# Computing, reading and storing the last block of 128 tokens in two column halves

## The chip, the cores and the metric

The kernel runs on one core of one Trainium2 chip. The metric is the device time of one execution in microseconds (us); lower is better. Times are medians of several executions. A ratio of two kernels is the mean time of one kernel's fast runs over the mean of the other's fast runs of the same rounds, so it is not quite the ratio of the medians quoted. "Same" means within 2%. All timed runs here were in the fast state, so nothing below depends on a slow run. Three runs (e6 to e8) are single looks (one profiled run), which are of unknown state for one core; they are used only for the order and the times of events in the last six microseconds.

In this kernel TensorE does the matmuls and writes the sums to PSUM, VectorE reads them from there, and SyncE issues the stores to memory (DMA transfers). A store moves as packets, and a semaphore, a counter that an engine can wait for, is raised after them: the last store of the kernel before is 128 packets of 2 KB, the last of which ended at 1052.30 us; 16 increments of its semaphore landed from 1052.70 to 1053.04. The "granted clock" in the views below is the share of TensorE's full clock that it was granted.

## The reference, cut to what matters

An attention with a feature map gives `x` (4608 tokens of 512 numbers). A mixture of 8 experts follows, and every token goes through all 8, weighted by a balanced table `P`:

```python
out = np.zeros((N, D), dtype=np.float32)         # N=4608, D=512
for e in range(E):                               # E=8 experts, hidden size 1024
    h = np.maximum(x @ w1[e], 0.0)
    ye = h @ w2[e]
    out += P[:, e:e + 1] * ye
```

The change concerns the last `h @ w2[7]`, of the last group of 512 tokens, and there only the last 128 tokens.

## The kernel before

Tokens are worked in nine groups of 512. For expert 7 the order is group 8, then 0 to 7, so group 7 is the last one. For it alone the second product is computed by plain matmuls in four blocks of 128 tokens. Each block is eight matmuls of 128x512 that sum into one bank of PSUM (a `P1` tile of the program, 128x512 FP32), one read by VectorE (`acc = P * bank + acc`), and one store of 256 KB. `pe`, `dve` and `dma` record an operation with an estimated duration and the keys that it reads and writes; a small planner orders the recorded operations, and the framework places the waits.

```python
# ... cut: attention, routing, the fast products of all other groups
    def store(g, ts, one=0):
        if one:
            dma('SP', 1 << 18, 320, lambda: nc.sync.dma_start(
                out=out[g * S:g * S + SM].rearrange('(p j) d -> p j d', j=NJ)[:, ts:ts + 1],
                in_=acc[g][:, ts:ts + 1, :]),
                [('acc', g, ts, j) for j in range(2)], [('out', g, ts)])
        # ... cut: stores of the other groups

    def down8(e, g, hT, w2):

        for ts in (2, 3, 0, 1):
            py = new("P1")                      # a P1 tile in PSUM, 512 columns
            for fc in range(8):
                i, j = fc // 4, ts // 2
                pe(512, lambda py=py, ts=ts, fc=fc: mm(
                    py(), hT[fc // 4]()[:, fc % 4, ts * 128:ts * 128 + 128], w2()[:, fc, :],
                    fc == 0, fc == 7), [...], [py])
            dve(580, lambda py=py, ts=ts: nc.vector.scalar_tensor_tensor(
                out=acc[g][:, ts, :], in0=py(), scalar=P[:, 4 * g + ts, e:e + 1],
                in1=acc[g][:, ts, :], op0=ALU.mult, op1=ALU.add),
                [py, "P"], [("acc", g, ts, j) for j in range(2)])
            store(g, ts, 1)
```

Here `NJ` is 4 and `SM` is 512. In the group's part of the output, partition `p` of block `ts` holds token `4p + ts`. A store of one block therefore writes 128 rows of 2 KB that lie 8 KB apart.

Of the kernel before, what the change touches and what calls it, by code (L numbers as in the profile page):

```python
# [12 lines left out]
ALU = mybir.AluOpType  # L13
# [155 lines left out]
def kernel(  # L169
# [11 lines left out]
    nc = tc.nc  # L181

    B, H, S, D = q.shape
    DF = w_phi.shape[1]
    N, DD = out.shape
    E = moe_w_gate.shape[1]
    FF = moe_w1.shape[2]
    NP = H // 2
    NJ = 4
    SM = 128 * NJ  # L190
# [19 lines left out]
    P = const.tile([128, NT, E], FP32, name="P")  # L210

    NA = 5
    acc = [accp.tile([128, 4, DD], FP32, name=f"acc{g}", tag=f"acc{g}") for g in range(NA)]
# [16 lines left out]
    def pe(cols, fn, r=(), w=(), takes=()):  # L230
        plan.op("PE", max(cols / 2400.0 + 0.0025, 0.032), 0.32, fn, r, w, takes)
# [4 lines left out]
    def dve(el, fn, r=(), w=(), shared=False):  # L236
        plan.op("DVE", el / 960.0 + 0.09, 0.22, fn, r, w, shared=shared)
# [4 lines left out]
    def dma(queue, nbytes, rate, fn, r=(), w=()):  # L242

        plan.op(queue, 0.8 if queue == "POOL" else 0.6, 0.0, fn, r, w, (), nbytes / rate / (125 / 100))
# [43 lines left out]
    def new(tag):  # L288
        return R[tag].new()
# [6 lines left out]
    def load_w(e, r=()):  # L296
        w1, w2 = new("w1"), new("w2")
        for w, src in ((w1, moe_w1), (w2, moe_w2)):
            dma("POOL", 2 << 20, 280, lambda w=w, src=src: nc.gpsimd.dma_start(
                out=w(), in_=src[e].rearrange("(c p) f -> p c f", p=128)),  # L300
                r, [(w, i, j) for i in range(2) for j in range(2)])
        return w1, w2
# [80 lines left out]
    def mm(out_, lhsT, rhs, start, stop):  # L383
        nc.tensor.matmul(out_, lhsT=lhsT, rhs=rhs, start=start, stop=stop)  # L384
# [341 lines left out]
    for i in range(2):  # L726
        dve(64, lambda i=i: nc.vector.tensor_copy(
            out=wphi2[64 * i:64 * i + 64, i, :], in_=wphi_f[64 * i:64 * i + 64, :]),
# [10 lines left out]
    for i in range(2):  # L739
# [5 lines left out]
        out=wgate, in_=moe_w_gate.rearrange("(c p) e -> p c e", p=128)), w=["wgate"])  # L745
# [126 lines left out]
        expert0(i)  # L872


    def store(g, ts, one=0):
        if one:
            dma('SP', 1 << 18, 320, lambda: nc.sync.dma_start(
                out=out[g * S:g * S + SM].rearrange('(p j) d -> p j d', j=NJ)[:, ts:ts + 1],
                in_=acc[g][:, ts:ts + 1, :]),
                [('acc', g, ts, j) for j in range(2)], [('out', g, ts)])  # L880
        elif g < 8:
            if ts % 2:
                dma("SP", 1 << 19, 320, lambda: nc.sync.dma_start(
                    out=out[g * S:g * S + SM].rearrange("(p j) d -> p j d", j=NJ)
                    [:, ts - 1:ts + 1], in_=acc[g][:, ts - 1:ts + 1, :]),
                    [("acc", g, t, j) for t in (ts - 1, ts) for j in range(2)], [("out", g, ts)])
        else:
            for i in range(2):
                b = 2 * ts + i
                rows = slice(i * 64, i * 64 + 64)  # L890
                dma("SP", 1 << 17, 320, lambda b=b, rows=rows: nc.sync.dma_start(
                    out=out[b * S + SM:(b + 1) * S], in_=acc[8][rows, ts, :]),
                    [("acc", 8, ts, j) for j in range(2)], [("out", 8, b)])
# [9 lines left out]
    def sub(eng, el, out_, x, y, op, r, w):  # L903
        f = nc.vector if eng is dve else nc.gpsimd
        kw = {"shared": True} if eng is dve else {}
        eng(el * 0.6 if eng is dve else el * 1.04 + 128,
            lambda: f.tensor_tensor(out=out_(), in0=x(), in1=y(), op=op), r, w, **kw)  # L907

    def sums_w(e, w1, w2):

        eng = pool if e == 0 else dve

        def q(w, i, j):
            if w is w1:
                return lambda: w1()[:, 2 * j:2 * j + 2, 512 * i:512 * i + 512]
            return lambda: w2()[:, 4 * i:4 * i + 4, 256 * j:256 * j + 256]

        def k(w, i, j):
            return [(w, i, j)] if e else [(w, n) for n in range(4)]

        S = [None] + [new("T") for _ in range(3)]
        T = [None] + [new("T") for _ in range(3)]

        def s(n):
            return lambda: S[n]().rearrange("p (a b) -> p a b", a=2)

        def t(n):
            return lambda: T[n]().rearrange("p (a b) -> p a b", a=4)


        a11, a12, a21, a22 = (1, 0), (1, 1), (0, 0), (0, 1)
        late = ["late"] + (["P"] if e == 1 else [])
        sub(eng, 1024, s(2), q(w1, *a11), q(w1, *a21), ALU.subtract,
            k(w1, *a11) + k(w1, *a21) + late, [S[2]])
        sub(eng, 1024, q(w1, *a21), q(w1, *a21), q(w1, *a22), ALU.add,
            k(w1, *a22) + late, k(w1, *a21))
        sub(eng, 1024, s(1), q(w1, *a21), q(w1, *a11), ALU.subtract,
            k(w1, *a21) + k(w1, *a11) + late, [S[1]])
        sub(eng, 1024, s(3), q(w1, *a12), s(1), ALU.subtract,
            k(w1, *a12) + [S[1]] + late, [S[3]])  # L940
        b11, b12, b21, b22 = (0, 0), (0, 1), (1, 0), (1, 1)
        sub(eng, 1024, t(2), q(w2, *b22), q(w2, *b12), ALU.subtract,
            k(w2, *b22) + k(w2, *b12) + late, [T[2]])
        t1, t1k = q(w2, *b12), k(w2, *b12)
        if 1 and e == E - 1:
            T[0] = new("T")
            t1, t1k = t(0), [T[0]]
        sub(eng, 1024, t1, q(w2, *b12), q(w2, *b11), ALU.subtract,
            k(w2, *b11) + k(w2, *b12) + late, t1k)
        sub(eng, 1024, t(1), q(w2, *b22), t1, ALU.subtract, k(w2, *b22) + t1k + late, [T[1]])  # L950
        sub(eng, 1024, t(3), q(w2, *b21), t(1), ALU.subtract,
            k(w2, *b21) + [T[1]] + late, [T[3]])
        A = {"11": (q(w1, *a11), k(w1, *a11)), "12": (q(w1, *a12), k(w1, *a12)),
             "22": (q(w1, *a22), k(w1, *a22)), "s1": (q(w1, *a21), k(w1, *a21)),
             "s2": (s(1), [S[1]]), "s3": (s(2), [S[2]]), "s4": (s(3), [S[3]])}
        Bq = {"11": (q(w2, *b11), k(w2, *b11)), "21": (q(w2, *b21), k(w2, *b21)),
              "22": (q(w2, *b22), k(w2, *b22)), "t1": (t1, t1k),
              "t2": (t(1), [T[1]]), "t3": (t(2), [T[2]]), "t4": (t(3), [T[3]])}
        return A, Bq
# [118 lines left out]

    def down8(e, g, hT, w2):

        for ts in (2, 3, 0, 1):
            py = new("P1")
            for fc in range(8):
                i, j = fc // 4, ts // 2
                pe(512, lambda py=py, ts=ts, fc=fc: mm(
                    py(), hT[fc // 4]()[:, fc % 4, ts * 128:ts * 128 + 128], w2()[:, fc, :],
                    fc == 0, fc == 7), [(hT[i], fp, j) for i in range(2) for fp in range(2)]
                    + [(w2, i, j) for i in range(2) for j in range(2)] + ["P"], [py])
            dve(580, lambda py=py, ts=ts: nc.vector.scalar_tensor_tensor(
                out=acc[g][:, ts, :], in0=py(), scalar=P[:, 4 * g + ts, e:e + 1],  # L1090
                in1=acc[g][:, ts, :], op0=ALU.mult, op1=ALU.add),
                [py, "P"], [("acc", g, ts, j) for j in range(2)])
            store(g, ts, 1)

    def down7(e, g, hT, B7):

# [107 lines left out]
    ORDER = "X1 x10 w10 x11 X2 x20 y10 x21 Z1 y11 X3 w11 x30 x31 x40 x41 w20 Y1 w21 X4 Z2".split()  # L1204
    dn = None
    for e in range(0 if 0 else 1, E):
        w1, w2 = load_w(e, [("xT", 5, 3)]) if e else W[0]
        if e == (0 if 0 else 1):
            for g in (0,1,2,3,4,5,6,7,8):
                sums_x(g)  # L1210
        A7, B7 = sums_w(e, w1, w2)
        for g in (range(0, NG) if e == 0 else range(NG) if e < E - 1 else [8, *range(8)]):
            X = load_x(g)
            hT = [new("hT") for _ in range(2)]
            un = up7(A7, g, X, hT, ["up0"])
            for n in ORDER:
                if len(n) == 3:
                    un[n[:2], int(n[2])]()
                elif dn is not None:
                    dn[n]()  # L1220
            if dn is not None:
                dn["out"]()
            if 1 and e == E - 1 and g == 7:
                down8(e, g, hT, w2)
            else:
                dn = down7(e, g, hT, B7)
    if not 1:
        for n in ORDER:
            if len(n) == 2:
                dn[n]()  # L1230
        dn["out"]()
    plan.run(tc)


# [28 lines left out]
```

## Time and profile before

| What | us |
|---|---|
| median of the first three runs | 1054.22 (1053.27 to 1054.75) |
| span of the profiled run | 1054.02 |
| start of the last block's first matmul | 1047.93 |
| from there to the end: "the drain" | 6.09 |

First lines of the page, before: the span, busy time of each engine with its share and its number of instructions, and the shares by engine of the chain of work that ended last.

```profile
span 1054.0 us, 24517 instructions
...
PE 1022.4 (97%) x9512; PEld 841.3 (80%) x9512; DVE 824.6 (78%) x1634; ACT 707.8 (67%) x1560; POOL 475.4 (45%) x551
...
PE 89%; ACT 4%; DVE 3%; DMA 2%; POOL 1%; issue 1%; DVEq 0%; ACTq 0%; POOLq 0%
```

TensorE bounds the kernel as a whole: busy 97% of the span, 89% of the chain. The change leaves TensorE's work alone and aims at what follows it. So the place to read is the end of the chain, in order of time (start, duration, what):

```profile
1046.37 1.73 PE P_16349 L384 x8
1048.10 1.74 PE P_16360 L384 x8
1049.84 0.02 issue
1049.86 0.75 DVE acc_4739 L1089
```

The chain counts a matmul from where the one before it ended, which is why the last block stands at 1048.10 here and starts at 1047.93 in the trace. The chain's view stops at the last engine instruction; the store and the final waits come after it. The timeline of the same stretch (start, duration, engine, line, operation; in brackets the idle time before it and what ended it):

```profile
1047.93 1.89 PE L384 MATMUL P_16360<-w_13336,hT 128*128 128x512 bf16 x8
1047.94 1.39 PEld L384 LDWEIGHTS <-hT 128*128 128x128 bf16 x7
1048.20 0.75 DVE L1089 SCALAR_TENSOR_TENSOR acc_4739<-P_16349,P,acc_4739 128x512 f32<-128x512 f32 x1 [1.04 <-PE P_16349 L384]
1048.98 1.99 SPq L877 DMA_DIRECT2D out_dram<-acc_4739  x2
1049.86 0.75 DVE L1089 SCALAR_TENSOR_TENSOR acc_4739<-P_16360,P,acc_4739 128x512 f32<-128x512 f32 x1 [0.91 <-PE P_16360 L384]
```

The line of SyncE's queue merges two issues of 0.33 us each, at 1048.98 and at 1050.64, and the time between them. Cutting the drain at the events of the trace gives this view (a stretch with its length, busy time of each engine with instructions in brackets, granted clock, DMA share, GB/s):

```profile
1047.93:1049.82 1.89, 1.89 (x9) 0.69 (x7) 0.75 (x1) 0.00 (x0) 0.00 (x0) 1.00 0.38 140
1049.82:1050.64 0.82, 0.00 (x1) 0.00 (x0) 0.75 (x1) 0.00 (x0) 0.00 (x0) 1.00 0.84 317
1050.64:1051.46 0.82, 0.00 (x0) 0.00 (x0) 0.00 (x0) 0.00 (x0) 0.00 (x0) 1.00 0.00 0
1051.46:1052.31 0.85, 0.00 (x0) 0.00 (x0) 0.00 (x0) 0.00 (x0) 0.00 (x0) 1.00 0.82 308
1052.31:1053.04 0.73, 0.00 (x0) 0.00 (x0) 0.00 (x0) 0.00 (x0) 0.00 (x0) 1.00 0.00 0
1053.04:1054.02 0.98, 0.00 (x0) 0.00 (x0) 0.00 (x0) 0.00 (x0) 0.00 (x0) 0.52 0.00 0
```

Read it as six steps: matmuls; VectorE's read (the DMA traffic here is still the store of the block before); nothing moves for 0.82 us after the issue; the last 256 KB move; nothing moves for 0.73 us until the last of the store's 16 semaphore increments lands; final waits. No step overlaps another. Only a shorter step, or a smaller last piece, can make the drain shorter.

### The profile page before, as it was taken

The numbers are of one execution on the slowest core, as the hardware profiler recorded it, in microseconds if no ns is written. First come the engines' busy times: TensorE is split into PE (matmuls) and PEld (weight loads), VectorE is DVE, ScalarE is ACT, GpSimd is POOL, SyncE is SP. The second block draws the span as 40 slices with busy tenths as digits, with TensorE's granted clock in tenths as the row PEclk, the third lists the DMA queues.
The fourth block names the chain that finished last, engine by engine and source line by source line (L and its number), as shares of the span: only waits on it lengthen the run. The fifth ranks groups of instructions, "written<-read, shape, count | busy, mean of one in ns | idle before, by whom it ended". The sixth has DMA issues, their size and how long they took to land.

```text
span 1054.0 us, 24517 instructions
## 1 busy us (share of the span) xinstructions
PE 1022.4 (97%) x9512; PEld 841.3 (80%) x9512; DVE 824.6 (78%) x1634; ACT 707.8 (67%) x1560; POOL 475.4 (45%) x551
## 2 busy tenths in 40 slices
PE   5889999999899999999999999999999999999998
PEld 3546666654588888888888888888888888888886
DVE  6889988988867787778877787778777877777775
ACT  5789989954896656666666666665666666666663
POOL 8776755510044344334444444444333544434442
PEclk9899999999999999999999999999999999999999
DMA  9998886914511133113411341116111521114333
GB/s 143 141 187 133 136 142 121 159 47 164 101 41 47 48 89 81 41 51 81 89 43 41 76 86 42 49 46 127 41 41 51 111 61 42 41 41 128 114 131 120
DMA packets 105236, 91.57 MB, mean 87 GB/s; under 512 B 45344, under 2 KB 80288, under 8 KB 105120
## 3 DMA queue, kind: packets, MB, share of 16 engines
q1 hardware_dynamic: 65040, 63.78, 22.3%
q0 software_dynamic: 40080, 26.23, 18.2%
q8 instruction: 74, 1.21, 0.5%
q14 instruction: 42, 0.34, 0.1%
HBM read 94.98 MB, written 14.16 MB: 104 GB/s over the span
## 4 chain that ended last, share of the span: by engine, by line
PE 89%; ACT 4%; DVE 3%; DMA 2%; POOL 1%; issue 1%; DVEq 0%; ACTq 0%; POOLq 0%
DVE m L376 1%; DMA qkT<-qk 1%; ACT U L1027 1%; DMA qk_r<-in_q_dram 1%; DVE xb L590 0%; PE P_13550 L999 0%; PE P_12438 L999 0%; PE P_8591 L999 0%; PE P_15513 L999 0%; PE P_14556 L999 0%; PE P_14095 L999 0%; PE P_13743 L999 0%; PE P_13392 L999 0%; PE P_13188 L999 0%; PE P_12788 L999 0%
## 5 line engine op out<-in xcount | busy, mean ns | idle before, releaser
L999 PEld LDWEIGHTS <-S 128*128 128x128 bf16 x1984 | 194.1, 98 | 22.9 <-issue 0.5
L999 PEld LDWEIGHTS <-T 128*128 128x128 bf16 x1512 | 147.9, 98 | 20.4 <-issue 3.2
L999 PEld LDWEIGHTS <-hT 128*128 128x128 bf16 x1488 | 145.6, 98 | 16.9
L907 DVE TENSOR_TENSOR S<-hT 128x1024 bf16<-128x1024 bf16 x124 | 80.3, 684 | 0.0
L1155 POOL TENSOR_TENSOR acc_77<-acc_77,V 128x512 f32<-128x512 f32 x28 | 36.3, 1308 | 54.6 <-ACT V L1152 54.5
L1155 POOL TENSOR_TENSOR acc_78<-acc_78,V 128x512 f32<-128x512 f32 x28 | 37.4, 1349 | 49.0 <-ACT V L1152 48.9
L1155 POOL TENSOR_TENSOR acc_81<-acc_81,V 128x512 f32<-128x512 f32 x28 | 35.6, 1276 | 51.0 <-ACT V L1152 50.5
L1155 POOL TENSOR_TENSOR acc_4738<-acc_4738,V 128x512 f32<-128x512 f32 x28 | 35.5, 1274 | 51.1 <-ACT V L1152 50.5
L1155 POOL TENSOR_TENSOR acc_4740<-acc_4740,V 128x512 f32<-128x512 f32 x28 | 35.2, 1268 | 51.3 <-ACT V L1152 51.2
L1155 POOL TENSOR_TENSOR acc_80<-acc_80,V 128x512 f32<-128x512 f32 x28 | 35.4, 1269 | 49.9 <-ACT V L1152 49.3
L1155 POOL TENSOR_TENSOR acc_4737<-acc_4737,V 128x512 f32<-128x512 f32 x28 | 35.6, 1277 | 49.0 <-ACT V L1152 48.4
L1155 POOL TENSOR_TENSOR acc_79<-acc_79,V 128x512 f32<-128x512 f32 x28 | 35.8, 1289 | 48.1 <-ACT V L1152 47.6
L384 PEld LDWEIGHTS <-hT 128*128 128x128 bf16 x320 | 30.7, 101 | 26.6 <-issue 2.2
L1155 POOL TENSOR_TENSOR acc_4739<-acc_4739,V 128x512 f32<-128x512 f32 x24 | 30.4, 1273 | 37.3 <-ACT V L1152 36.9
L384 PEld LDWEIGHTS <-w_449 128*128 128x128 bf16 x288 | 26.1, 98 | 24.0 <-issue 2.9
L907 DVE TENSOR_TENSOR S<-S,hT 128x1024 bf16<-128x1024 bf16 x62 | 42.5, 685 | 0.8
L907 DVE TENSOR_TENSOR S<-hT,S 128x1024 bf16<-128x1024 bf16 x62 | 42.3, 682 | 0.0
L384 PEld LDWEIGHTS <-qkT 128*128 128x128 bf16 x256 | 24.4, 102 | 20.6 <-DVE xb_r L595 4.4
L999 PEld LDWEIGHTS <-w_3831 128*128 128x128 bf16 x288 | 28.2, 98 | 4.2 <-issue 0.7
L999 PEld LDWEIGHTS <-w_13099 128*128 128x128 bf16 x288 | 28.2, 98 | 3.3
L999 PEld LDWEIGHTS <-w_11515 128*128 128x128 bf16 x288 | 28.2, 98 | 3.3
L999 PEld LDWEIGHTS <-w_5153 128*128 128x128 bf16 x288 | 28.2, 98 | 3.3
(4017 smaller groups left out, 3296.2 us busy)
## 6 DMA issues: line engine op xcount, KB each, us to landing
v_m<-in_v_dram SPq DMA_DIRECT2D x15, 512.0 KB, 5.4
qk<-in_k_dram POOLq DMA_DIRECT2D x15, 256.0 KB, 5.1
qk<-in_q_dram POOLq DMA_DIRECT2D x15, 256.0 KB, 5.8
X<-xd_98 SPq DMA_DIRECT2D x7, 256.0 KB, 2.6
X<-xd_99 SPq DMA_DIRECT2D x7, 256.0 KB, 2.7
X<-xd_100 SPq DMA_DIRECT2D x7, 256.0 KB, 2.7
X<-xd_101 SPq DMA_DIRECT2D x7, 256.0 KB, 3.1
X<-xd_102 SPq DMA_DIRECT2D x7, 256.0 KB, 2.6
```

Source lines behind the costliest of these rows:

```text
L376: dve(el, lambda: nc.vector.tensor_reduce(out=dst(), in_=src(), axis=AX.X, op=ALU.max, apply_absolute_value=True), r, w)
L384: nc.tensor.matmul(out_, lhsT=lhsT, rhs=rhs, start=start, stop=stop)
L907: lambda: f.tensor_tensor(out=out_(), in0=x(), in1=y(), op=op), r, w, **kw)
L999: pe(256, lambda i=i, k=k, z=z: nc.tensor.matmul(bank()[:, 256 * i:256 * i + 256], lhsT=lhs(k, i), rhs=rhs(k), start=first and z, stop=k = ...
L1027: act(512, lambda: nc.scalar.copy(out=u[fp][n]().rearrange("p a b -> p (a b)"), in_=x[fp]()), [x[fp]], [u[fp][n]])
L1155: pool(670, lambda: nc.gpsimd.tensor_tensor(out=acc[g][:, 2 * i:2 * i + 2, 256 * j:256 * j + 256], in0=acc[g][:, 2 * i:2 * i + 2, 256 * j: ...
```

## The change

The intent is a smaller last piece. The last block is cut into columns 0 to 255 and 256 to 511. Each half has its own PSUM bank, its own read and its own store of 128 KB (128 rows of 1 KB). The first half is read and stored while TensorE computes the second.

```diff
-        for ts in (2, 3, 0, 1):
-            py = new("P1")
-            for fc in range(8):
-                ...
-            dve(580, ... acc[g][:, ts, :] = P * py + acc[g][:, ts, :] ...)
-            store(g, ts, 1)
+        for ts in (2, 3, 0, 1):
+            for cols in ([slice(0, 512)] if ts != 1 else [slice(0, 256), slice(256, 512)]):
+                py = new("P1")
+                n = cols.stop - cols.start
+                for fc in range(8):
+                    i, j = fc // 4, ts // 2
+                    pe(n, lambda py=py, ts=ts, fc=fc, n=n, cols=cols: mm(
+                        py()[:, 0:n], hT[fc // 4]()[:, fc % 4, ts * 128:ts * 128 + 128],
+                        w2()[:, fc, cols], fc == 0, fc == 7), [...], [py])
+                keys = [("acc", g, ts, j) for j in range(2) if n == 512 or j == cols.start // 256]
+                dve(n + 70, lambda ...: nc.vector.scalar_tensor_tensor(
+                    out=acc[g][:, ts, cols], in0=py()[:, 0:n], scalar=P[:, 4 * g + ts, e:e + 1],
+                    in1=acc[g][:, ts, cols], op0=ALU.mult, op1=ALU.add), [py, "P"], keys)
+                dma("SP", n << 9, 320, lambda ts=ts, cols=cols: nc.sync.dma_start(
+                    out=out[g * S:g * S + SM].rearrange("(p j) d -> p j d", j=NJ)[:, ts, cols],
+                    in_=acc[g][:, ts, cols]), keys, [("out", g, ts, cols.start)])
```

The rest of the diff (cut) takes out the now unused branch of `store` and some dead conditions.

More of the change, by code (lines that the diff above doesn't have):

```diff
@@ L872, with store @@
         expert0(i)
-    def store(g, ts, one=0):
-        if one:
-            dma('SP', 1 << 18, 320, lambda: nc.sync.dma_start(
-                out=out[g * S:g * S + SM].rearrange('(p j) d -> p j d', j=NJ)[:, ts:ts + 1],
-                in_=acc[g][:, ts:ts + 1, :]),
-                [('acc', g, ts, j) for j in range(2)], [('out', g, ts)])
-        elif g < 8:
+    def store(g, ts):
+        if g < 8:
             if ts % 2:
@@ L944, in sums_w @@
         t1, t1k = q(w2, *b12), k(w2, *b12)
-        if 1 and e == E - 1:
+        if e == E - 1:
             T[0] = new("T")
@@ L1081, in down8 @@
         for ts in (2, 3, 0, 1):
-            py = new("P1")
-            for fc in range(8):
-                i, j = fc // 4, ts // 2
-                pe(512, lambda py=py, ts=ts, fc=fc: mm(
-                    py(), hT[fc // 4]()[:, fc % 4, ts * 128:ts * 128 + 128], w2()[:, fc, :],
-                    fc == 0, fc == 7), [(hT[i], fp, j) for i in range(2) for fp in range(2)]
-                    + [(w2, i, j) for i in range(2) for j in range(2)] + ["P"], [py])
-            dve(580, lambda py=py, ts=ts: nc.vector.scalar_tensor_tensor(
-                out=acc[g][:, ts, :], in0=py(), scalar=P[:, 4 * g + ts, e:e + 1],
-                in1=acc[g][:, ts, :], op0=ALU.mult, op1=ALU.add),
-                [py, "P"], [("acc", g, ts, j) for j in range(2)])
-            store(g, ts, 1)
+            for cols in ([slice(0, 512)] if ts != 1 else [slice(0, 256), slice(256, 512)]):
[5 more added lines that the diff above has]
+                        py()[:, 0:n], hT[fc // 4]()[:, fc % 4, ts * 128:ts * 128 + 128],
+                        w2()[:, fc, cols], fc == 0, fc == 7),
+                        [(hT[i], fp, j) for i in range(2) for fp in range(2)]
+                        + [(w2, i, j) for i in range(2) for j in range(2)] + ["P"], [py])
+                keys = [("acc", g, ts, j) for j in range(2) if n == 512 or j == cols.start // 256]
+                dve(n + 70, lambda py=py, ts=ts, n=n, cols=cols: nc.vector.scalar_tensor_tensor(
+                    out=acc[g][:, ts, cols], in0=py()[:, 0:n], scalar=P[:, 4 * g + ts, e:e + 1],
[3 more added lines that the diff above has]
+                    in_=acc[g][:, ts, cols]), keys, [("out", g, ts, cols.start)])
     def down7(e, g, hT, B7):
@@ L1222 @@
                 dn["out"]()
-            if 1 and e == E - 1 and g == 7:
+            if e == E - 1 and g == 7:
                 down8(e, g, hT, w2)
@@ L1226 @@
                 dn = down7(e, g, hT, B7)
-    if not 1:
-        for n in ORDER:
-            if len(n) == 2:
-                dn[n]()
-        dn["out"]()
     plan.run(tc)
```

## The prediction

> What bounds the kernel. By the page's table of engines TensorE is busy 97% of the 1054.0 us span, VectorE 78%; the chain of work that ended last is 89% TensorE. The change touches only the final block of 128 tokens, so only the drain after the last matmul counts.
>
> The drain now, from the timeline and the chain from 1042 us on. Four blocks of eight 128x512 matmuls run back to back, 1.73 us each, the last from 1048.10 to 1049.84. VectorE reads it in 0.751 us. The 256 KB store is issued at 1050.64; its packets move from 1051.47 to 1052.31; its last semaphore increment lands at 1053.04; 0.98 us of final waits and drains follow, to 1054.02. The store before it moves 1049.81 to 1050.65. So 4.2 us lie after the last matmul, and nothing overlaps them.
>
> The change. The block becomes two halves of eight 128x256 matmuls, each with its own PSUM bank, read and 128 KB store.
> - TensorE: eight more matmuls and weight loads. The 128x256 products just before run at 0.87 us per eight, so two halves take 1.74 us against 1.73: +0.01 us. [...] 98 ns loads do not disturb the 109 ns pace.
> - VectorE: the first half's read runs under the second half's matmuls. The second half's takes about 0.48 us (128x256 reads of the same form, by shape) instead of 0.751: -0.27 us, on the critical path.
> - Store: the first half should be issued near 1049.5 and be moved by about 1051.1, before the second half's packets can begin (issue near 1050.37, plus the 0.83 us from issue to first packet of the last two stores: 1051.2). SyncE needs about 0.4 us per issue, so the extra issue delays nothing. Packets of 1 KB on this queue take 46 to 49 ns against 84 ns for 2 KB (other transfers of this trace), so I estimate 0.5 to 0.6 us of moving against 0.84: -0.25 us. The issue and landing costs (0.83 and 0.74 us) stay. [...] here 0.74 us follow the last packet.
> - Final waits: the last store's semaphore may become the last one tested, worth 0.06 us.
>
> Sum: about -0.5 us of 1054, less than the 1.5 us between the three runs of before. I predict 1053.7 us, 8 in 10 within 1052.4 to 1055.0. Faster by over 2%: 0.5%; within 2%: 99%; slower by over 2%: 0.5%.
>
> What would show it. The last block's matmuls take 1.74 us; last read about 0.48 us; two stores of 128 KB about 0.9 us apart; the last one's data finished within 0.6 us of its first packet; from the end of the last matmul to the end of the span 3.7 us instead of 4.2.
>
> What would make it wrong. If 1 KB rows cost as much as 2 KB ones or queue behind the first half, only 0.3 us remain; if the first store delays the second's issue, perhaps zero. [...]

The sum: 0.01 - 0.27 - 0.25 - 0.06 = -0.57 us, stated as about -0.5.

## The result

| | before | after |
|---|---|---|
| median, six runs each | 1053.35 (1051.75 to 1054.75) | 1053.05 (1052.42 to 1054.12) |
| ratio | | 0.9997, 95% interval 0.9984 to 1.001 |
| drain of the profiled run | 6.09 | 5.27 |

(The median of before with six runs takes in the three runs quoted above.) The time lies within the predicted range. The timed runs can't tell whether anything was gained, because the interval is 2.6 thousandths wide, about 2.7 us. The profiles can. The page of after:

```profile
span 1050.9 us, 24536 instructions
...
PE 1019.2 (97%) x9520; PEld 839.5 (80%) x9520; DVE 824.3 (78%) x1635; ACT 708.4 (67%) x1560; POOL 476.2 (45%) x551
...
PE 88%; ACT 3%; DVE 2%; DMA 1%; issue 1%; POOL 1%; ACTq 0%; DVEq 0%
```

There are 8 more matmuls and one more VectorE instruction, as there should be. The end of its chain, and its timeline from the last block on:

```profile
1042.94 4.57 PE P L384 x29
1047.51 0.03 issue
1047.54 0.48 DVE acc L1089
```

```profile
1045.15 2.34 PE L384 MATMUL P<-w,hT 128*128 128x512 bf16 x18
1045.59 1.63 PEld L384 LDWEIGHTS <-hT 128*128 128x128 bf16 x15
1045.86 1.29 DVE L1089 SCALAR_TENSOR_TENSOR acc<-P,P,acc 128x512 f32<-128x512 f32 x2 [1.04 <-PE P L384]
1046.64 1.74 SPq L1092 DMA_DIRECT2D out_dram<-acc  x3
1047.54 0.48 DVE L1089 SCALAR_TENSOR_TENSOR acc<-P,P,acc 128x256 f32<-128x256 f32 x1 [0.39 <-PE P L384]
```

The merged lines hide a little: "x18" are two 128x512 matmuls and sixteen of 128x256, and "x2" are the block before's read and the first half's. The last read takes 0.48 us where it took 0.75. The six steps of the drain after:

```profile
1045.59:1047.49 1.90, 1.90 (x17) 1.47 (x15) 1.24 (x2) 0.00 (x0) 0.00 (x0) 1.00 0.39 144
1047.49:1048.05 0.56, 0.01 (x1) 0.00 (x0) 0.48 (x1) 0.00 (x0) 0.00 (x0) 1.00 0.98 366
1048.05:1048.87 0.82, 0.00 (x0) 0.00 (x0) 0.00 (x0) 0.00 (x0) 0.00 (x0) 1.00 0.67 215
1048.87:1049.39 0.52, 0.00 (x0) 0.00 (x0) 0.00 (x0) 0.00 (x0) 0.00 (x0) 1.00 0.74 252
1049.39:1049.94 0.55, 0.00 (x0) 0.00 (x0) 0.00 (x0) 0.00 (x0) 0.00 (x0) 1.00 0.00 0
1049.94:1050.86 0.92, 0.00 (x0) 0.00 (x0) 0.00 (x0) 0.00 (x0) 0.00 (x0) 0.91 0.00 0
```

Taking the same steps from the trace's single records (start of the last block's first matmul = 0):

| step | before | after | difference |
|---|---|---|---|
| last block's matmuls, to the end of the stream | 1.727 | 1.746 | +0.02 |
| to the start of the last read | 0.201 | 0.203 | 0 |
| last read | 0.751 | 0.485 | -0.27 |
| end of read to issue of the store | 0.028 | 0.028 | 0 |
| issue to first packet | 0.826 | 0.826 | 0 |
| first packet to end of the last packet | 0.833 | 0.513 | -0.32 |
| last packet to last semaphore increment | 0.741 | 0.549 | -0.19 |
| to the end of the span | 0.983 | 0.922 | -0.06 |
| drain | 6.090 | 5.272 | -0.82 |

**The rest of the span is chance.** The profiled spans differ by 3.17 us, and 0.82 us of that is the drain. The other 2.35 us lie before it. Comparing VectorE's instructions one by one, the sixtieth starts at 35.19 us before and at 32.76 us after, and the distance stays between 2.43 and 2.33 us up to the last block. Up to there each compute engine has the same instructions in the same order in both programs. The stretch from 0 to 40 us of before, then of after (columns as above; the clock is the number after POOL's):

```profile
0.00:40.00 40.00, 27.06 (x260) 17.92 (x261) 29.46 (x72) 26.51 (x67) 31.28 (x59) 0.91 0.88 136
```

```profile
0.00:40.00 40.00, 26.19 (x285) 16.86 (x286) 31.40 (x78) 28.27 (x75) 32.57 (x61) 1.00 0.97 152
```

After got more instructions done in the same 40 us. The granted clock was lower in the profile of before, but it is not a full account: a second profile of after (e2 below) had a granted clock of 1.00 in this stretch as well and reached the last block 1.4 us later than the first one. The kernel before wanders as much with itself: its second profile (e1 below) reached the last block 2.44 us earlier than its first. What makes the first 40 us vary was not tested. Whoever reads 3.2 us of gain off the two spans reads mostly noise.

### The profile page after: what moved, and what is told of

Its sections match the earlier page's. It is cut to its first block, busy times and chain, and to the rows that moved or that the text cites. A ratio compares the mean times of both kernels' runs of the same rounds, so it can differ in the third digit from the quotient of the medians.

```text
span 1050.9 us, 24536 instructions
## 1 busy us (share of the span) xinstructions
PE 1019.2 (97%) x9520; PEld 839.5 (80%) x9520; DVE 824.3 (78%) x1635; ACT 708.4 (67%) x1560; POOL 476.2 (45%) x551
## 4 chain that ended last, share of the span: by engine, by line
PE 88%; ACT 3%; DVE 2%; DMA 1%; issue 1%; POOL 1%; ACTq 0%; DVEq 0%
PE P L994 70%; PE P L384 16%; ACT acc L1163 2%; PE P L570 1%; DMA qkT<-qk 1%; DVE m L376 1%; ACT U L1022 1%; PE P L609 1%; ACT V L1153 0%; DVE xb L590 0%; DVE P L582 0%; DVE m_r L376 0%; PE P L575 0%; ACT hT L1031 0%; POOL qk_r L367 0%
## 5 line engine op out<-in xcount | busy, mean ns | idle before, releaser
L1156 POOL TENSOR_TENSOR acc<-acc,V 128x512 f32<-128x512 f32 x248 | 317.6, 1289 | 440.8 <-ACT V L1153 437.5
L1026 DVE CUSTOM_DVE_ANT_0 hT<-P,U 128x512 bf16<-128x512 f32 x378 | 255.5, 688 | 127.2 <-ACT U L1022 77.4
L1022 ACT COPY U<-P 128x512 f32<-128x512 f32 x378 | 217.3, 589 | 125.3 <-PE P L994 120.4
L1153 ACT ACTIVATE V<-P,P 128x256 f32<-128x256 f32 x496 | 205.9, 475 | 133.3 <-PE P L994 132.6
L994 PEld LDWEIGHTS <-w 128*128 128x128 bf16 x2016 | 197.3, 98 | 23.7 <-issue 0.7
L1141 DVE SCALAR_TENSOR_TENSOR acc<-P,P,acc 128x256 f32<-128x256 f32 x372 | 159.4, 478 | 56.0 <-PE P L994 53.3
L994 PE MATMUL P<-X,w 128*128 128x256 bf16 x1008 | 154.4, 273 | 0.5 <-ACT U L1022 0.5
L994 PE MATMUL P<-X,T 128*128 128x256 bf16 x1008 | 148.6, 273 | 2.6 <-ACT U L1022 2.5
L994 PE MATMUL P<-xT,w 128*128 128x256 bf16 x1008 | 150.4, 273 | 0.0
L994 PE MATMUL P<-w,hT 128*128 128x256 bf16 x992 | 142.9, 273 | 0.0
```

The source lines that it names most:

```text
L994: pe(256, lambda i=i, k=k, z=z: nc.tensor.matmul(bank()[:, 256 * i:256 * i + 256], lhsT=lhs(k, i), rhs=rhs(k), start=first and z, stop=k = ...
L1022: act(512, lambda: nc.scalar.copy(out=u[fp][n]().rearrange("p a b -> p (a b)"), in_=x[fp]()), [x[fp]], [u[fp][n]])
L1026: dve(500, lambda: nc.vector._custom_dve(ADD_SAT, out=out_(fp, i, j), in0=bank[fp]().rearrange("p (a b) -> p a b", a=2), in1=u[fp][n](), s ...
L1141: dve(330, lambda n=n, ts=ts: nc.vector.scalar_tensor_tensor(out=acc[g][:, ts, 256 * j:256 * j + 256], in0=bank()[:, 256 * n:256 * n + 256 ...
L1153: act(390, lambda n=n: nc.scalar.activation(out=u()[:, n, :], in_=bank()[:, 256 * n:256 * n + 256], func=ACT.Copy, bias=0.0, scale=P[:, 4 ...
L1156: pool(670, lambda: nc.gpsimd.tensor_tensor(out=acc[g][:, 2 * i:2 * i + 2, 256 * j:256 * j + 256], in0=acc[g][:, 2 * i:2 * i + 2, 256 * j: ...
```

## The experiments

The theory to test: the gain is 0.82 us, the sum of a shorter last read (0.27), a smaller last store (0.32 moving, 0.19 landing) and 0.06 of final waits, less 0.02 that the matmuls take longer. The rivals: it is chance; only one of the parts counts; the landing time follows something other than the size of the store. Four of the runs were made on one chip, four on a second and four on a third, each beside the kernel before. Correct results unless said otherwise. For e3, e4, e7, e11 and e12 the block was rewritten with three helpers: `mms` (eight matmuls), `read` (VectorE's instruction) and `put` (a store); the diffs of these runs are cut and show the edit in that form, e3 against after, e4 and e11 against before, e7 against e4, e12 against e11.

### e1 and e2: both kernels once more

No edit.

> The kernel before, unchanged. Theory: the drain, from the start of the last block's first matmul to the end of the span, was 6.09 us in the first profile and repeats to 0.05 us. The rest of the span may differ by 2 to 3 us, as the first profiles of before and after differed by 2.4 us at the thirty-fifth microsecond already, where the two programs are the same. Ratio of the times 1.000 with an interval no narrower than 0.0005. Rival: the drain itself varies by several tenths from run to run, so the 0.8 us seen between the two first profiles is chance; then it comes out outside 6.0 to 6.2.

> The kernel after, unchanged. Theory: the drain repeats the 5.27 us of its first profile to 0.05 us, 0.8 us less than before, while the ratio of the times, about 0.9992 by that, stays within what the spread of runs can hide (same). Rival, chance: a drain nearer 6 us.

| | median | ratio to before | drain |
|---|---|---|---|
| e1, before again | 1054.48 | 1.0000 (0.9987 to 1.0012) | 6.07 |
| e2, after again | 1054.27 | 0.9995 (0.9983 to 1.0008) | 5.27 |

The drains repeat to 0.02 us while the spans wander by microseconds. The difference of 0.80 us is not chance. The theory's ratio of about 0.9992 lies in the interval, and so does 1. Timed runs of this kernel can't settle it, and a single number off a profile can, provided it is the number of the stretch that the change touches.

### e3: halves for compute and read, one store

```diff
         for h in (A, B):                 # columns 0:256, 256:512
             py = mms(1, h)
             read(1, h, py)
-            put(1, h)
+        put(1, C)                        # one store of 512 columns
```

> The block is computed and read in two halves, but stored as before in one 256 KB store. Theory (the gain is a sum of a shorter read, -0.27 us, and a smaller last store, -0.33 moving, -0.19 landing and -0.06 in the final waits): the drain is 6.09 - 0.27 + 0.02 = 5.84 us. Rival (only the store counts, the read is hidden or made up for elsewhere): 6.09. Rival (all of the gain comes from the read, the store's parts are chance): 5.3.

Drain 5.83 us (ratio 0.9995, same). The theory said 5.84. The store behaved as before: 0.83 us to the first packet, 0.82 moving, 0.74 landing, 0.97 to the end. Its last read and its stores, from the timeline and the DMA view of the stretch (sizes, median us to landing):

```profile
1048.71 0.48 DVE L1094 SCALAR_TENSOR_TENSOR acc<-P,P,acc 128x256 f32<-128x256 f32 x1 [0.39 <-PE P L384]
```

```profile
out_dram<-acc SPq DMA_DIRECT2D x2, 256.0 KB, 2.4
```

So the shorter read is worth its 0.25 us net on its own, and both one-part rivals fall. Between this run and after only the store differs: 5.83 against 5.27, so the store in halves is worth the other 0.56 us (landing 0.51 us earlier, final waits 0.05 shorter).

### e4: whole read, two stores

```diff
         py = mms(1, C)
         read(1, C, py)
-        put(1, C)
+        put(1, A)
+        put(1, B)
```

> The block is computed and read whole, and stored in two 128 KB stores issued one behind the other. The second is issued 0.38 us after where the one store was. Theory (a 128 KB store of 1 KB rows moves in 0.51 and lands 0.55 us after its last packet whatever went before): last landing 0.13 us earlier than before, final waits 0.06 shorter, drain 5.90 us. Rival (the landing follows all the bytes in flight, so 0.74 us as for 256 KB): drain 6.1 us or more. Either way splitting the store alone gains little; what it needs is a first half that leaves early.

Drain 6.04 us (ratio 0.9997, same), between the two. The second store was issued 0.38 us after the first, as expected. Both stores' packets moving, then landing:

```profile
1048.92:1049.95 1.03, 0.00 (x0) 0.00 (x0) 0.00 (x0) 0.00 (x0) 0.00 (x0) 1.00 0.76 255
1049.95:1050.51 0.56, 0.00 (x0) 0.00 (x0) 0.00 (x0) 0.00 (x0) 0.00 (x0) 1.00 0.00 0
```

The last increment landed 0.57 us after the last packet, near the theory's 0.55. But the first store's packets were still moving until 4.07 us after the block's start, when the second's could have begun (3.92, 0.83 after its issue), and the two took 1.02 us together, against 0.83 for one store of the same bytes in 2 KB rows. So the second's packets ended 0.12 us later than my 0.51 us of moving allowed, and the last landing, forecast 0.13 us earlier than before, came at 5.12 us, no earlier than before's 5.11. The 0.05 us gained are the final waits: the last store holds the semaphore that is tested last (see e9 and e10).

So this run does not refute the rival. From first packet to last increment the last 256 KB took 1.59 us here, 1.57 in before and in e3 and 1.61 in e5, however the time divides between moving and landing; the last 128 KB of after took 1.06. So of the store's part of the gain the sum of 0.51 us is the safer number, and not its split into 0.32 of moving and 0.19 of landing. Cutting the store alone brought the last landing no earlier (5.12 us against 5.11). In after, where the first half leaves early, it came at 4.35.

### e5: 384 and 128 columns

```diff
-            for cols in ([slice(0, 512)] if ts != 1 else [slice(0, 256), slice(256, 512)]):
+            for cols in ([slice(0, 512)] if ts != 1 else [slice(0, 384), slice(384, 512)]):
 # ... cut: the keys of the read and the store follow the new columns
```

> The block is cut into 384 and 128 columns instead of 256 and 256, so the last piece is smaller still. Theory (the gain follows the size of the last piece, but TensorE pays for small pieces): eight 128-column matmuls cannot go faster than their weight loads of 98 ns, so TensorE needs about 8 x 162 + 8 x 100 = 2.10 us for the block, +0.35 us against halves; the last read is 0.13 us shorter (0.35 us), moving perhaps 0.1 to 0.15 and landing up to 0.1 shorter. Drain 5.2 to 5.4 us, no better than 5.27 of halves. Rival (smaller is always better, the matmuls pace with their columns): 128-column matmuls at 55 ns, the block 1.75 us, drain 4.9 to 5.0 us.

Drain 5.50 us (ratio 0.9999, same): worse than halves, but not for my reason. The 128-column matmuls kept pace with their columns (256 columns took 109 ns in after, 512 took 216 in before). In the stretch of the eight of them (0.45 us from the first start to the last block's end of stream) TensorE needed 56 ns for each:

```profile
1047.27:1047.72 0.45, 0.45 (x10) 0.43 (x7) 0.25 (x1) 0.00 (x0) 0.00 (x0) 1.00 0.00 0
```

The weight loads are recorded with 98 ns each, one starting every 56 ns, so they overlap one another; taking 98 ns as a floor for the pace was my error. The trace shows the loss behind the larger first piece. VectorE took 0.62 us for its read and was still at it when the last matmuls were done, so the last read began at 2.04 us, 0.29 us after the end of the stream instead of 0.20. And SyncE issued the last store at 2.57 us, 0.17 us after its data was ready (2.40), because it had the first piece's store to issue at 2.15. Then 256 KB moved in one go, and landing took 0.71 us. In this run the last piece's cost depended on the piece ahead of it: 0.09 us at the read and 0.17 at the issue.

### e6: the last store from ScalarE's queue

```diff
-                dma("SP", n << 9, 320, lambda ts=ts, cols=cols: nc.sync.dma_start(
+                last = cols.start == 256
+                eng = nc.scalar if last else nc.sync
+                dma("ACT" if last else "SP", n << 9, 320, lambda ts=ts, cols=cols, eng=eng: eng.dma_start(
```

> As after, but the last half's store is issued by the idle ScalarE's queue instead of SyncE's. Theory: SyncE was free when the last store came due, and the 0.83 us from issue to first packet are of the DMA and not of the issuing engine: drain 5.27 us, the same to 0.05. Rival (the second store waits behind the first one on SyncE or in its queue): drain shorter by 0.1 us or more.

Drain 5.30 us. As expected within the 0.05; SyncE was not in the way. The DMA view of its last stretch:

```profile
out_dram<-acc SPq DMA_DIRECT2D x1, 128.0 KB, 2.2
out_dram<-acc ACTq DMA_DIRECT2D x1, 128.0 KB, 1.9
```

The first half takes 2.2 us, with the block before's 256 KB still moving when it is issued (in e12 below, with no other store near by, first halves take 1.88 in the median); the last half takes 1.9 us from issue to landing, from either engine.

### e7: two stores by tokens (inconclusive)

```diff
-        put(1, A)
-        put(1, B)
+        for rows in (slice(0, 64), slice(64, 128)):
+            dma("SP", 1 << 17, 320, lambda rows=rows: nc.sync.dma_start(
+                out=out[g * S:g * S + SM].rearrange("(p j) d -> p j d", j=NJ)[rows, 1, :],
+                in_=acc[g][rows, 1, :]), keys(1, C), [("out", g, 1, rows.start)])
```

> As e4_two_stores, but the two stores cut the block by tokens: 64 rows of 2 KB each instead of 128 rows of 1 KB, the same 128 KB. It asks what the time from last packet to last increment follows. If the bytes of the store: 0.55 us, as in e4_two_stores. If the length of the rows: 0.74 us, as with the 256 KB store of 2 KB rows. Issues of 64-row stores took 0.6 us from one to the next earlier in the trace, so the second is issued near 3.3 us after the block's start; drain 6.1 us by bytes, 6.3 by row length.

Drain 6.50 us, landing 0.34 us. Neither of the expectations came out. The stores themselves were slow: a packet of 2 KB took 155 ns in the median against 84 elsewhere, and the 256 KB took 1.40 us instead of 0.83. When the packets come that slowly, the time after the last one says nothing about the faster stores. Why they came slowly was not sought. What it does show is that cutting a store by tokens is no substitute: it cost 0.4 us against one store.

### e8: the last half to consecutive memory (result wrong)

```diff
                 dma("SP", n << 9, 320, lambda ts=ts, cols=cols: nc.sync.dma_start(
                     out=out[g * S:g * S + SM].rearrange("(p j) d -> p j d", j=NJ)[:, ts, cols]
+                    if cols.start == 0 else out[0:64].rearrange("r (h d) -> (r h) d", h=2),
```

> As after, but the last half's store goes, wrongly on purpose, to 128 KB of consecutive memory (the first 64 rows of the output), instead of 1 KB pieces 8 KB apart. Result wrong in half a block and in those rows. If landing is slow because the pieces lie 8 KB apart: 0.36 us from last packet to last increment, as after the stores of 64 consecutive rows at 962 us, and a drain of 5.08 us. If only the number of bytes or of packets matters: 0.55 us and 5.27 us, unchanged.

Drain 5.08 us. The moving took the same 0.51 us, the landing 0.35 instead of 0.55:

```profile
1049.29:1049.81 0.52, 0.00 (x0) 0.00 (x0) 0.00 (x0) 0.00 (x0) 0.00 (x0) 1.00 0.74 252
1049.81:1050.16 0.35, 0.00 (x0) 0.00 (x0) 0.00 (x0) 0.00 (x0) 0.00 (x0) 1.00 0.00 0
```

With bytes, packets and their length unchanged, where the rows lie in memory decides 0.20 us of the landing, in this one look. 0.35 us of landing remain. Whether the 8 KB spacing or the other place in the output makes the difference was not tested, and no run shows what happens in these 0.20 us. Nor do the bytes of the last store alone set the landing: in e5 (0.71) and e9 (0.66, below) a last store of only 64 KB, with others right before it, landed later after its last packet than after's 128 KB (0.55). A layout that stores consecutive rows would need another assignment of tokens to partitions from the loads on, and was not tried.

### e9 and e10: smaller pieces

```diff
-            for cols in ([slice(0, 512)] if ts != 1 else [slice(0, 256), slice(256, 512)]):
+            for cols in ([slice(0, 512)] if ts != 1                                            # e9
+                         else [slice(0, 256), slice(256, 384), slice(384, 512)]):
+            for cols in ([slice(0, 512)] if ts > 1 else [slice(0, 256), slice(256, 512)] if ts == 0   # e10
+                         else [slice(0, 256), slice(256, 384), slice(384, 512)]):
```

> The block cut into 256, 128 and 128 columns. In e5_384_128 the 128-column matmuls went at 56 ns each, so TensorE pays nothing for the last two pieces; what spoilt e5 was that the 384-column piece was read late (0.62 us) and held back the last read and SyncE. Theory: the last read starts about 1.96 us after the block's start and takes 0.34, its store goes out near 2.36, its packets near 3.2 to 3.6, landing after 0.45 to 0.55 more: drain 5.0 to 5.2 us against 5.27. Rival (the stores in flight before it, 448 KB in two microseconds, hold the last 64 KB back): 5.25 us or more.

> As e9, and the block before it is cut into two halves of 256 columns too, so that half of its 256 KB leaves 0.87 us earlier and the queue is emptier when the last pieces come. Theory: if e9 is held back by the stores before it, this frees it: drain 4.9 to 5.0 us; if e9 was not held back, the same as e9 to 0.05. The time stays within 2% of before either way.

| | after | e9 | e10 |
|---|---|---|---|
| median; ratio to before | 1053.05; 0.9997 | 1054.16; 0.9999 | 1054.66; 1.0000 |
| last read ends | 2.43 | 2.32 | 2.32 |
| last store issued | 2.46 | 2.50 | 2.49 |
| last packet ends | 3.80 | 3.75 | 3.75 |
| last increment lands | 4.35 | 4.41 | 4.21 |
| end of the span (drain) | 5.27 | 5.76 | 5.49 |

Both missed. The last read did end 0.11 us earlier. SyncE then ate that: it was still at its earlier issues, and the last store went out at 2.50 and 2.49 us instead of 2.35. In e9, where 448 KB of other stores moved right before them without a pause, the last 64 KB landed 0.66 us after their packets; in e10, with those spread out, 0.46 us, and the last landing was 0.14 us earlier than in after. That fits the rival of e9 in part. But e10 still ended later, and the cause is in the last step: 1.28 us from the last increment to the end, and 1.35 in e9, where after has 0.92. The records of SyncE show it. From the traces (start in us, what SyncE waits for):

```text
after                          e10
1049.408  semaphore 115        1049.831  semaphore 108
1049.953  semaphore 116 <- last store   1050.272  semaphore 109 <- last store
1050.018  drain                1050.336  semaphore 111
                               1050.398  semaphore 112
                               1050.457  semaphore 113
                               1050.519  semaphore 114
                               1050.578  semaphore 115
                               1050.640  semaphore 116
                               1050.705  drain
```

At the end of these programs SyncE tests the DMA semaphores one by one in rising order, 62 ns each. Stores take the semaphores in turn (112 to 115 for the last four of before). In after the last store happens to hold 116, the last one tested, so all other tests are done by the time it lands. In e10 it holds 109 and six tests still follow (6 x 0.062 = 0.37 us; the step is 0.35 longer). In e9 it holds 108 with seven to follow (0.43; measured 0.43). In before it holds 115, one to follow, which is the 0.06 us of the theory. An e10 whose last store held 116 would drain in about 4.21 + 0.92 = 5.13 us, an estimate from these two traces, 0.14 us better than after. It was not run.

### e11 and e12: the last block forty times over (results wrong)

To see the gain in timed runs, the block's compute, read and store are put in a chain of 40 passes. Each waits for the store before it.

```diff
+        for rep in range(40):
+            X = ["gate"] if rep else []
             for h in (C,):               # e11;  (A, B) in e12
                 py = mms(1, h, X)
                 read(1, h, py)
                 put(1, h)
+            if rep < 39:
+                # twelve 128x512 dummy matmuls into a bank of their own, so that TensorE stays at work
+                dve(2, ... tensor_copy(out=acc[g][:, 1, 0:512:256], in_=P[:, 0, 0:2]), [], keys(1, C))
+                dve(1, ... tensor_copy(out=hT[0]()[:, 0, 128:129], in_=acc[g][:, 1, 0:1]),
+                    keys(1, C), [(hT[0], 0, 0), "gate"])
```

> The last block of the kernel before, computed, read and stored 40 times over, each pass starting only when the store of the pass before has landed (a small copy waits for it and rewrites one column of a matmul operand); twelve dummy matmuls in each pass keep TensorE at work meanwhile. Result wrong on purpose. Theory: a pass takes what the drain shows, 1.73 + 0.2 + 0.75 + 0.03 + 2.40 us and about 0.5 for the gate, near 5.6 us; the kernel takes about 1054 + 39 x 5.6 = 1272 us.

> The same chain of 40 passes with the block in two halves as in the kernel after. Result wrong on purpose. Theory: a pass is 0.27 - 0.02 + 0.51 = 0.76 us shorter than in e11_chain_whole (shorter read; a 128 KB store lands 1.89 us after its issue instead of 2.40), so 40 passes are 30 us shorter, near 1242 us: ratio to e11_chain_whole 0.976, plain in timed runs. Rival (the gain in the two first profiles, or a part of it, is an accident of that place in the program): less than half of that.

| | median | ratio to before | median pass in the trace |
|---|---|---|---|
| e11, whole | 1271.83 (1270.34 to 1272.12) | 1.2061 (1.2045 to 1.2078) | 5.52 |
| e12, halves | 1247.99 (1246.42 to 1251.50) | 1.1843 (1.1826 to 1.1859) | 4.89 |

The gate, put at about 0.5 us, took 0.42 us in the timeline of e11 from the start of its first copy to the next pass's first matmul (1106.49 to 1106.91). Forty passes are 23.8 us shorter, 0.60 us each; the intervals are far apart. This is the gain of the cut in timed runs, in a chain and not at the kernel's end, and the rival (less than half of 0.76) falls. It is also a fifth smaller than I had said. The lines of `acc` over the passes, e11 then e12 (duration min/median/max in ns; the last line is the stores' time to landing, in e12 of first and second halves together):

```profile
L1094 DVE SCALAR_TENSOR_TENSOR acc<-P,P,acc x37: 749/750/752, 1064.8 to 1264.5; 128x512 f32<-128x512 f32 x37
...
DMA to landing us min/median/max: 2.3/2.3/3.0
```

```profile
L1094 DVE SCALAR_TENSOR_TENSOR acc<-P,P,acc x73: 482/483/485, 1062.3 to 1241.1; 128x256 f32<-128x256 f32 x73
...
DMA to landing us min/median/max: 1.9/1.9/3.8
```

The read gives its 0.27 us in every pass. In the median the whole store lands after 2.29 us in the chain, not 2.40, and the second half after 1.88, near the 1.89 of after, so the store gives 0.41 us instead of 0.51: 0.27 - 0.02 + 0.41 = 0.66, against 0.63 between the median passes. So what is smaller than in the kernel is the whole store's time to landing. In the chain no other block's store is near by, in the kernel there is one; whether that is the reason was not tested.

## Why the prediction was right or wrong

- **Outcome.** Right: 1053.7 us was predicted, 1053.05 measured, within the range and within 2%. With a noise of about a microsecond that alone proves little: 1053.7 was reckoned down from the 1054.22 of before's first three runs, and before's own median of six runs is 1053.35, so the kernel before would have hit the range too. The parts below are the test.
- **TensorE, +0.01 us.** Measured +0.02 us. In the trace of after, twice as many loads of 98 ns left the 128x256 matmuls at 109 ns each, about half the 216 ns of the 128x512 ones before.
- **Read, -0.27 us.** Measured -0.27 us, on the critical path, as e3 shows by itself. Right.
- **First half out of the way in time.** It was to be moved before the second half's packets start: its packets end at 3.13 us after the block's start, the second half's begin at 3.29. Right, and e4 shows what happens otherwise: the last landing comes no earlier than with one store.
- **Moving, -0.25 us.** Measured -0.32 us: 0.51 us, inside the stated 0.5 to 0.6.
- **Landing, "The issue and landing costs (0.83 and 0.74 us) stay."** This is the mis-sized term. The issue cost stayed (0.83). The landing fell to 0.55 us, a further -0.19 us. That it would stay at half the size was my assumption, and no trace had shown it. It does not hold here: 0.74 us for before's 256 KB, 0.55 for 128 KB, 0.35 for the same 128 KB in consecutive rows (e8). What sets these times stays open.
- **Final waits, -0.06 us.** Measured -0.06 us, by the mechanism named: no test of 62 ns is left after the landing, where before had one; e9 and e10 show the same thing with the sign turned.
- **Sum.** About -0.5 us was stated; the listed terms add to -0.57; measured -0.82, of which -0.19 is landing and -0.07 is moving. From the end of the last matmul's record to the end of the span 3.7 us were expected instead of 4.2; it was 3.36.
- **Noise.** The gain was expected to be less than the 1.5 us between the three runs of before. So it was: the timed runs do not show it, and the first two profiles' spans would even have shown 3.2 us, four times the gain.

## What to carry to other kernels

This kernel is bound by one engine to its end, and what came after that engine's last instruction, 4.20 us before and 3.36 after, was a chain of steps without overlap. A smaller last piece shortened some of them: with half the piece the read (0.75 to 0.48 us), the moving (0.83 to 0.51) and the landing (0.74 to 0.55) all got shorter, the 0.83 us from issue to first packet did not, and TensorE paid 0.02 us for it. Where a trace shows such a chain, cut the last piece until the piece ahead of it, the issue interval (on SyncE 0.38 us in e4, 0.42 in e5) or the order of the final semaphore tests (62 ns each) takes the gain back; halves were the best of the cuts run here. Judge such a change by the stretch that it touches, which repeated to 0.02 us, or by repeating that stretch in a chain, and not by a total that wanders by 2 us.
